# A four-column-tile form for projection and mixer matmuls that follow value matmuls, with a planned order, in a two-layer attention-and-mixer kernel

## The chip, the cores and the metric

The kernel runs on one core of one Trainium2 chip. The time is device microseconds of one execution, and lower is better. Each profile gives the granted clock of TensorE (PE). PE multiplies matrices, ACT (ScalarE) evaluates exponentials and gelus, DVE (VectorE) copies and normalises, and the program gives each engine its own queue of instructions. Where the text below says "at equal clock", it compares single runs of two kernels whose granted clocks are nearly the same.

## The reference, cut to what matters

```python
x = A_x                                           # 1 x 2048 x 448
x = x + attention(layernorm(x), wqkv, wo)         # 16 heads of 28
x = x + B(layernorm(x), w1, w2, w3, w4)
x = x + attention(layernorm(x), wqkv, wo)         # same weights again
x = x + B(layernorm(x), w1, w2, w3, w4)

# B: h = gelu(layernorm(x) @ w1); four quarters of h shifted by +1, -1, +2, -2 rows;
#    x1 = x + shifted(h) @ w2;  x1 + gelu(layernorm(x1) @ w3) @ w4     (w3: 448 x 1792)
```

The softmax needs 2 x 16 x 2048 x 2048 exponentials. They are ACT's work and the largest single item of the kernel.

## The kernel before

The program writes tasks (Python generators); a scheduler picks, operation by operation, what each engine does next, and so fixes the order of every engine's queue before anything runs. Rows of x go in 16 tiles of 128. The scores of a "granule" (3 or 2 banks of PSUM, alternately) are computed by PE, one exponential instruction turns them into the tile PT, and value matmuls multiply PT with V. Scores for granule n+2 can start only after exponential n has read its banks.

Score matmuls use tiles of 32 rows of the array, value matmuls tiles of 32 columns, and all other matmuls the whole array ("plain"):

```python
# scores: contraction over 32 rows, tile at row r0
yield op("pe", ..., lambda e, ...: e.matmul(out=ps[:, bk, :], lhsT=kT[r0:r0 + rn, g, kc:kc + 128],
    rhs=qT[r0:r0 + rn, g, q0:q0 + 512], ..., tile_position=(r0, 0)), ..., mode="r%d" % rn, dl=0.55)
# values: four heads j, 32 columns each
yield op("pe", ..., lambda e, ...: e.matmul(out=ps[32 * j:32 * j + 32, UBK, 0:128 * nt],
    lhsT=vaug[:, vs, 32 * (4 * g + j):32 * (4 * g + j) + 32], rhs=rhs, ..., tile_position=(0, 32 * j)), ..., mode="col4")
# a mixer matmul, plain: w3
for (fc, rows) in KCM:
    yield op("pe", c_mm(NW), lambda e, ...: e.matmul(out=ps[:, bi(b), 0:NW],
        lhsT=w3[0:rows, fc, 128 * fch:128 * fch + 128], rhs=xt.v[0:rows, 0:n, fc, :], ...), ...)
```

The greedy rule, with fixed priorities, and the fillers. A filler is a plain matmul whose result nobody reads. It is put where the scheduler expects PE to be idle, so that PE keeps its clock (e10 below, with 330 fillers fewer than after, spent 109 us at half clock against 20):

```python
key = (ready if eng == "act" else start, t[0], t[1])      # earliest start, then task priority
# ... cut ...
def keep_pe_busy(self, until):
    while self.cur["pe"] + dur + 0.12 < until:            # dur = 0.13: ident @ wv, 256 columns
        # ... cut: a free bank, at most 80% busy over the last 4 us ...
        self.P.add("pe", lambda e, b=pick: fn(e, b), reads, [key(pick)], t_end=t + dur)
```

The shifted quarters are kept in hT, a ring of 8 tiles. A mixer task for tile t may write its slot when the tile that held it is done with. "Done" is signalled only at the end of that tile's whole mixer:

```python
def t_mixA(L, tiles, direct):
    for t in tiles:
        for tp in (t - HR - 1, t - HR, t - HR + 1):       # HR = 8
            if 0 <= tp < NT:
                yield ("wait", ("mixBt", L, tp))
# t_x1: ps = shifted(hT) @ w2: the last reader of hT.   Then w3, gelu, w4, and only then
                yield ("sig", ("x2", L, t))
                yield ("sig", ("mixBt", L, t))
```

## Time and profile before

| what | before |
|---|---|
| time, median (4 runs) | 1169.1 us (1163.9 to 1169.3) |
| span of the profiled run | 1167.1 us, granted clock 0.980 |
| ACT busy / idle | 1047.7 / 119.4 us |
| exponentials | 821 instructions, 940.2 us |
| first exponential starts / last one ends | 27.9 / 1080.9 us |
| PE busy, of which fillers | 1091.1, 168.2 us |

From the page of the kernel before: busy time of the engines with share of the span and number of instructions, then three rows of the span in 40 slices (tenths busy; PEclk is the granted clock in tenths).

```profile
PE 1091.1 (93%) x7799; PEld 406.0 (35%) x7799; DVE 649.7 (56%) x1566; ACT 1047.7 (90%) x955; POOL 58.4 (5%) x76
PE   4899999989999999998999999998999999899998
ACT  5799999999999999994999999998889999999144
PEclk9999999999999999999999999998779999999999
```

PE looks like the busiest engine, but its busy time contains fillers, as the group of line 1302 shows. In a group's line the columns are: line, engine, operation, output and inputs, count, busy time and mean ns of one, idle time of the engine just before and what ended it.

```profile
L955 ACT ACTIVATE PT<-ps 128x1536 bf16<-128x1536 f32 (+1 forms) x821 | 940.2, 1258 | 45.9 <-PE ps L932 37.7
L1302 PE MATMUL ps<-wv,ident 128*128 128x256 bf16 x1102 | 168.2, 279 | 8.8 <-DVE kT L704 2.2
```

So ACT sets the floor, and its idle time is what can be won. The table by stage of the kernel before, cut at the first and at the last exponential, shows where that time lies: us from the span's start and length, then the busy time (and count) of each engine, the clock, DMA share and GB/s.

```profile
0.00:27.90 27.90, 12.27 (x73) 4.67 (x73) 21.31 (x82) 13.99 (x21) 12.13 (x18) 1.00 0.76 177
27.90:1080.90 1053.00, 1000.05 (x7110) 350.81 (x7109) 578.04 (x1356) 1005.84 (x875) 40.29 (x47) 0.98 0.12 31
1080.90:1167.10 86.20, 78.82 (x623) 50.55 (x617) 50.33 (x130) 27.90 (x61) 5.99 (x11) 1.00 0.11 30
```

ACT, the fourth engine in each row, is idle for 13.9 us ahead of the first exponential, about 47 us between the first and the last, and 58.3 us in the tail of 86.2 us. The largest gap in the middle is the change of layers. ACT's timeline there (start, length, what; in brackets the idle time before and what ended it):

```profile
539.18 0.60 ACT L955 ACTIVATE PT<-ps 128x512 bf16<-128x512 f32 x1
556.01 2.37 ACT L955 ACTIVATE PT<-ps 128x1024 bf16<-128x1024 f32 x2 [16.24 <-PE ps L932]
```

The tail is long because the mixer runs late. The chain that ended last, in order of time, still holds the w3 matmuls, the gelu and the w4 matmuls of tiles 7 to 10 after the last exponential:

```profile
1094.80 12.28 PE ps L1239 x56
...
1107.89 6.19 ACT h2T L1254
...
1114.12 10.77 PE ps L1259 x56
```

What a change of shape costs PE is read from the starts of its matmuls. A plain matmul of 512 columns is followed by the next after 216 ns. Where the next one is of another kind (row tiles, column tiles, plain), a further 95 to 105 ns pass, in every pairing. Leaving out pairs with one of the small matmuls of the softmax's normalisation, 1,807 such changes are in this trace: about 180 us of PE.

### The profile page before, as it was taken

What the parts mean: (1) busy time and instruction counts of PE and PEld (TensorE: products, weight loads), DVE (VectorE), ACT (ScalarE), POOL (GpSimd) and SP (SyncE); (2) the same over time, 40 slices, a digit from 0 to 9 for tenths busy, and PEclk for the clock granted to TensorE, in tenths of its full rate; (3) what the DMA queues carried; (4) which work ended last, traced back from release to release, by engine and by line L of the source; (5) the groups of instructions that cost most, each with busy time, mean ns of one, the idle gap of its engine ahead of it and who ended that gap; (6) DMA issues with size and microseconds to landing.
All of it is one profiled execution on the core that took longest, in us unless ns stands there. A gap on an engine that the chain in (4) does not pass through costs nothing.

```text
span 1167.1 us, 18576 instructions
## 1 busy us (share of the span) xinstructions
PE 1091.1 (93%) x7799; PEld 406.0 (35%) x7799; DVE 649.7 (56%) x1566; ACT 1047.7 (90%) x955; POOL 58.4 (5%) x76
## 2 busy tenths in 40 slices
PE   4899999989999999998999999998999999899998
PEld 1222333333332323334233323332333333333565
DVE  7876356523573255734767462557542574447952
ACT  5799999999999999994999999998889999999144
POOL 4000000000010000000001000000000010001000
PEclk9999999999999999999999999998779999999999
DMA  7122160000000000000111112321000110010011
GB/s 170 37 82 64 32 157 19 15 1 19 19 18 2 19 19 19 12 8 19 28 37 42 28 46 63 83 55 45 10 15 1 31 28 1 1 31 14 23 31 35
DMA packets 79213, 40.18 MB, mean 34 GB/s; under 512 B 63960, under 2 KB 72536, under 8 KB 79128
## 3 DMA queue, kind: packets, MB, share of 16 engines
q1 hardware_dynamic: 77544, 36.23, 12.2%
q0 software_dynamic: 1584, 2.75, 0.8%
q8 instruction: 61, 1.00, 0.3%
q14 instruction: 24, 0.20, 0.1%
HBM read 13.75 MB, written 8.13 MB: 19 GB/s over the span
## 4 chain that ended last, share of the span: by engine, by line
ACT 44%; PE 39%; DVE 14%; DMA 1%; issue 1%; POOL 0%; SPq 0%; DVEq 0%
ACT PT L955 38%; PE ps L932 9%; PE ps L979 7%; PE ps L1259 5%; PE ps L1239 4%; PE ps L1302 4%; ACT h2T L1254 4%; PE ps L695 3%; PE ps L756 2%; PE ps L1118 2%; DVE x1b L1194 1%; PE ps L715 1%; PE ps L1050 1%; DVE x_res L1197 1%; DVE st L1199 1%
## 5 line engine op out<-in xcount | busy, mean ns | idle before, releaser
L955 ACT ACTIVATE PT<-ps 128x1536 bf16<-128x1536 f32 (+1 forms) x821 | 940.2, 1258 | 45.9 <-PE ps L932 37.7
L932 PE MATMUL ps<-qT,kT 32*128 32x512 bf16 (+1 forms) x2048 | 335.8, 392 | 13.8 <-ACT PT L955 9.1
L979 PE MATMUL ps<-PT,vaug 128*32 128x512 bf16 (+1 forms) x2304 | 232.5, 368 | 3.1 <-ACT PT L955 1.8
L1302 PE MATMUL ps<-wv,ident 128*128 128x256 bf16 x1102 | 168.2, 279 | 8.8 <-DVE kT L704 2.2
L932 PEld LDWEIGHTS ps<-qT,kT 32*128 32x128 bf16 (+1 forms) x2048 | 79.4, 91 | 253.7 <-ACT PT L955 176.2
L1248 DVE CAST h2T<-ps 128x512 bf16<-128x512 f32 (+2 forms) x126 | 73.9, 586 | 113.0 <-PE ps L1239 112.2
L1239 PE MATMUL ps<-xT,w 128*128 128x512 bf16 (+3 forms) x672 | 129.0, 311 | 0.3
L1302 PEld LDWEIGHTS ps<-wv,ident 128*128 128x128 bf16 x1102 | 93.5, 99 | 82.3 <-issue 45.7
L1259 PE MATMUL ps<-w,h2T 128*128 128x448 bf16 x448 | 101.0, 358 | 11.4 <-ACT h2T L1254 11.4
L979 PEld LDWEIGHTS ps<-PT,vaug 128*32 128x32 bf16 x2304 | 57.2, 94 | 125.8 <-issue 88.6
L1262 DVE TENSOR_TENSOR x_res<-x_res,ps 128x448 f32<-128x448 f32 x32 | 19.8, 618 | 120.5 <-PE ps L1259 120.5
L1239 PEld LDWEIGHTS ps<-xT,w 128*128 128x128 bf16 x672 | 49.6, 97 | 58.4 <-issue 32.3
L1254 ACT ACTIVATE h2T<-h2T 128x7168 bf16<-128x7168 bf16 (+2 forms) x9 | 45.1, 5015 | 20.2 <-DVE h2T L1248 20.1
L1259 PEld LDWEIGHTS ps<-w,h2T 128*128 128x128 bf16 x448 | 38.7, 98 | 60.1 <-issue 19.5
L994 DVE COPY u_sb<-ps 128x512 f32<-128x512 f32 (+1 forms) x36 | 22.7, 629 | 37.1 <-PE ps L979 36.1
L1118 PE MATMUL ps<-xT,w 128*112 128x512 bf16 (+2 forms) x160 | 40.8, 364 | 0.6 <-DVE x1b L1194 0.6
L695 PE MATMUL ps<-xT,wk_pad 128*128 128x512 bf16 x128 | 39.8, 398 | 1.1 <-DVE qT L739 0.8
L695 PE MATMUL ps<-xT,wq_pad 128*128 128x512 bf16 (+1 forms) x144 | 38.6, 369 | 0.8 <-DVE qT L739 0.7
L1067 DVE TENSOR_SCALAR hT<-ps 112x512 f16<-112x512 f32 (+1 forms) x32 | 21.0, 655 | 31.0 <-PE ps L1118 31.0
L998 DVE SCALAR_TENSOR_TENSOR u_sb<-uin,fct,ps 128x512 f32<-128x512 f32 x24 | 17.9, 747 | 36.1 <-PE ps L979 34.2
L1050 PE MATMUL ps<-wo_pad,otn 128*128 128x448 bf16 x128 | 35.8, 362 | 2.0 <-DVE x_res L1054 1.3
L620 DVE BATCH_NORM_STATS2 st<-x_res 128x6 f32<-128x448 f32 x60 | 37.0, 618 | 1.0
(138 smaller groups left out, 852.0 us busy)
## 6 DMA issues: line engine op xcount, KB each, us to landing
uscr<-u_sb SPq DMA_DIRECT2D x24, 256.0 KB, 2.7
uin<-uscr SPq DMA_DIRECT2D x24, 256.0 KB, 2.8
x_res<-in_A_x_dram POOLq DMA_DIRECT2D x3, 896.0 KB, 12.0
out_dram<-uin SPq DMA_DIRECT2D x16, 112.0 KB, 1.7
w<-in_B_w_dram SPq DMA_DIRECT2D x1, 1568.0 KB, 15.6
w<-in_B_w_dram SPq DMA_DIRECT2D x1, 1344.0 KB, 10.7
h2T<-in_A_wqkv_dram SPq DMA_DIRECT2D x2, 336.0 KB, 6.5
xT<-xn SPq DMA_TRANSPOSE x37, 3.6
```

The lines of the kernel that those rows point to most:

```text
L620: yield op("dve", 0.55, lambda e: e.bn_stats(out=st6[:, t, :], in_=w4[:, t, :] if staged else x_res[:, t, :]), reads=[("w4",) if staged el ...
L695: yield op("pe", c_mm(nw), lambda e, fc=fc, rows=rows, b=b: e.matmul(out=ps[:, bi(b), 0:nw], lhsT=wpad[0:rows, fc, 128 * g:128 * g + 128], ...
L932: yield op("pe", 0.225 if k == 0 else 0.005 if nt == 4 or k == 1 else 0.215, lambda e, bk=bk, r0=r0, rn=rn, g=g, kc=kc, q0=q0: e.matmul(ou ...
L955: yield op("act", 0.077 + 0.427 * cnt, lambda e, b0=b0, p0=p0, cnt=cnt: e.activation(out=PT[:, p0:p0 + cnt, :], in_=ps[:, b0:b0 + cnt, :], ...
L979: yield op("pe", 0.055 if nt == 4 else 0.035, lambda e, j=j, rhs=rhs, vs=vs, i=i: e.matmul(out=ps[32 * j:32 * j + 32, UBK, 0:128 * nt], lh ...
L1050: yield op("pe", c_mm(D), lambda e, g=g, tt=tt, b=b: e.matmul(out=ps[:, bi(b), 0:D], lhsT=otn[:, g, 128 * tt:128 * tt + 128], rhs=wo_pad[: ...
L1118: yield op("pe", c_mm(NW), lambda e, fc=fc, rows=rows, grp=grp, b=b: e.matmul(out=ps[0:112, bi(b), 0:NW], lhsT=w1[0:rows, fc, 112 * grp:11 ...
L1239: yield op("pe", c_mm(NW), lambda e, fc=fc, rows=rows, fch=fch, b=b: e.matmul(out=ps[:, bi(b), 0:NW], lhsT=w3[0:rows, fc, 128 * fch:128 * ...
L1248: yield op("dve", c_ps(NW), lambda e, fch=fch, b=b: e.tensor_copy(out=h2T[:, fch, hoff:hoff + NW], in_=ps[:, bi(b), 0:NW]), reads=[("ps", ...
L1254: yield op("act", c_act(14 * NW), lambda e: e.activation(out=h2T[:, :, hoff:hoff + NW], in_=h2T[:, :, hoff:hoff + NW], func=ACT.Gelu_apprx ...
L1259: yield op("pe", c_mm(D), lambda e, fch=fch, i=i, b=b: e.matmul(out=ps[:, bi(b), 0:D], lhsT=h2T[:, fch, hoff + 128 * i:hoff + 128 * i + 12 ...
L1302: SC.fill = (0.13, lambda e, b: e.matmul(out=ps[:, bi(b), 0:256], lhsT=ident[:, :], rhs=wv[:, 0, 0:256], start=True, stop=True), ["b6", "b ...
```

## The change

Its stated intent: a projection or mixer matmul that follows a value matmul is issued as four matmuls of 32 columns each, in the four column tiles, so that the array's mode does not change. The difference between the two programs holds more than that:

1. the four-column form;
2. ring slots of hT that count as free once the x1 matmuls have been issued ("x1"), not after w4 ("mixBt");
3. projections and mixer matmuls split into independent tasks per group (`par`);
4. scores of the two-tile units in four 32-row tiles, where they used two 64-row tiles;
5. a plan: the schedule is built, latest starts are computed backwards, and it is built again with them as priorities, twice; then 193 fixed random perturbations of these priorities (the recorded texts below say 200; the list in the kernel has 193 numbers);
6. some changed duration constants and rules in the scheduler. Among them, a filler may use any of the eight PSUM banks that holds nothing live, where it had two banks.

The core of the diff, with cuts marked:

```diff
+        def mm(nw, m, dst, lhs, rhs, start, stop, **kw):
+            def whole(e):
+                return e.matmul(out=dst(0, m), lhsT=lhs(0, m), rhs=rhs, start=start, stop=stop)
+            def cols4(e):
+                return [e.matmul(out=dst(a, min(m, a + 32)), lhsT=lhs(a, min(m, a + 32)), rhs=rhs,
+                                 start=start, stop=stop, tile_position=(0, a)) for a in range(0, m, 32)]
+            return op("pe", c_mm(nw), whole, cols=cols4, **kw)
...
                         m = kw.get("mode", "plain")
+                        if self.pe_mode == "col4" and "cols" in kw:
+                            m, dur, fn = "col4", dur + self.COLT, kw["cols"]
...
-                key = (ready if eng == "act" else start, t[0], t[1])
+                key = (ready if eng == "act" else max(start, self.cur[eng] + self.EPS) if eng in ("pe", "dve") else start, ranks[k])
...
+    def latest_starts(self, total):      # cut: backwards over all operations
+def reorder(plan, seed):                 # cut: shifts some tasks of the plan by random amounts
...
-                        yield ("wait", ("mixBt", L, tp))
+                        yield ("wait", ("x1", L, tp))
...
-            for fch in range(14):
+            def w3_group(fch):
...
+            yield from par(prio, [w3_group(fch) for fch in range(14)])
...
+        plan = None
+        for k in range(ROUNDS):          # 2
+            res = attempt(plan)
+            plan = res[2].latest_starts(res[0])
+        for seed in SEEDS:               # 193 numbers
+            plan = reorder(plan, seed)
+        est, P, SC = attempt(plan)
```

## The prediction

> **What bounds the kernel now.** The page gives ACT 1047.7 us busy (90%) and PE 1091.1 us, but 168 us of PE are fillers, so ACT sets the floor: exponentials 940.2 us, gelu 45.1, tanh 20.1, direct gelus 11.6, table loads about 20. Its 119 us of idle time can be won. The ACT timeline places it: about 15 us before the first exponential (27.9 us); about 50 between that and the last (1081 us), of which 16.2 in one gap at 540 us between the layers, 11 at 803-870 us and 9 at 34-110 us; about 58 in the 86 us tail.
>
> **Why.** At 540 us and in the tail ACT waits for mixer work that ran late. In the chain that ended last the 4-tile gelu stands at 1108-1114 us, its second matmuls follow, and only their addition at 1117 us starts the last tiles' mixer. That is the ring of hT: slots come free by "mixBt", signalled after w4, although the x1 matmuls read hT last, long before. In the 803-870 us stretch the granted clock was 0.75 (table by stage).
>
> **Mode changes, from matmul starts.** Unchanged, a 512-column matmul follows after about 216 ns; a change of shape (32-row, four-column, plain) adds 95-105 ns in every pairing. The Trainium skill, "TensorEngine Tiling (Array Packing)", Key Properties, says that changing the mode drains the engine; the trace agrees and gives the size. I count about 1,800 changes, 180 us of PE. About 190 are between value and plain matmuls, about 100 between value matmuls and fillers; the rest enter or leave score matmuls and stay.
>
> **The change, costed.**
> - Four-column form: removes 190 x 0.1 = 19 us of PE, perhaps 25 with more work placed behind value matmuls. It costs about 12 ns a group (starts 3.5 ns apart): on some 500 matmuls, 6 us. Net 13-19 us of PE, mostly hidden behind ACT: worth about 5 us. The value matmuls already stream at 217 ns per group with 94 ns loads hidden, so I expect no load cost.
> - The last two units' scores use four 32-row tiles for two 64-row: about 10 us of PE off.
> - Slots freed at x1, independent groups, latest-start priorities from planned passes: mixer batches run beside attention in place of the 152 us of fillers outside the tail. Gap at 540: 16 to about 3 us. Other gaps 35 to about 22. Tail: the batch of tiles 7-10 (12.3 + 6.2 + 10.8 us in the chain) and part of the next leave it; the last three tiles remain, about 23 us of PE and 20 of latency: 86 to about 44 us. Moved gelus and table loads, about 12 us, delay the last exponential.
> - ACT work: unchanged.
>
> **Sum.** 1169 - 13 - 13 - 42 + 12 = about 1113; I say 1114 us, range 1090 to 1144. Faster by over 2% 0.90, within 2% 0.08, slower 0.02.
>
> **What would show each step.** ACT busy within 10 us of 1048, idle about 65. Last exponential 1060-1080 us; tail 40-50 us without a 4-tile gelu. Gap between layers below 6 us. Value-to-plain changes near zero; matmul instructions up by well over 1,000; filler time down by a third or more. One four-column group of 512 columns follows another after 215-230 ns.
>
> **What would make it wrong.** The order is tuned on modelled durations; where the chip differs, in-order queues turn small errors into ACT waits: 1130-1145. The clock halves where PE looks idle: fewer fillers, or narrow tiles counting as less activity, could bring more 0.75 stretches. If the mixer still lags, the tail stays. If four loads per group don't hide, crowded stretches slow. Better: in-stream idle near zero gives 1090.

## The result, and the profile after

The kernel after takes 1121.3 us (median of 4 runs, 1113.2 to 1121.6) against 1169.1: 48 us less. The ratio is 0.9585, with a 95% interval of 0.9534 to 0.9635. A ratio is the mean time of one kernel's runs over that of the other's of the same rounds, so it is not quite the ratio of the medians quoted. In another job (run e12 below) the same kernel took 1113.6 us.

The page of the kernel after, the same rows:

```profile
PE 1054.9 (94%) x9097; PEld 418.1 (37%) x9097; DVE 615.7 (55%) x1531; ACT 1053.1 (94%) x968; POOL 56.3 (5%) x76
PE   4999999999999999999999999999999999999998
ACT  4899999999999999998999999999999999989944
PEclk9999999999999999999999999999999999979999
```

ACT works as much as before (1053.1 us); its idle time fell from 119.4 to 66.7 us. The two groups that answer to those of before:

```profile
L1122 ACT ACTIVATE PT<-ps 128x1536 bf16<-128x1536 f32 (+1 forms) x821 | 937.3, 1254 | 16.3 <-PE ps L1096 9.1
L1475 PE MATMUL ps<-wv,ident 128*128 128x256 bf16 x1154 | 178.2, 280 | 4.0 <-DMA wv<-in_A_wqkv_dram 2.4
```

ACT's wait for scores fell from 37.7 to 9.1 us, while filler time rose a little. The table by stage of the kernel after, cut at its own first and last exponential (40.1 and 1070.7 us):

```profile
0.00:40.10 40.10, 24.80 (x138) 11.75 (x138) 28.82 (x99) 21.54 (x34) 13.95 (x20) 1.00 0.58 134
40.10:1070.70 1030.60, 987.63 (x8564) 377.56 (x8563) 558.75 (x1357) 1012.51 (x882) 37.88 (x48) 0.99 0.13 32
1070.70:1119.80 49.10, 42.42 (x399) 28.79 (x397) 28.08 (x77) 19.09 (x54) 4.48 (x8) 0.99 0.13 34
```

The sum is exact: the head is 12.2 us longer, the middle 22.4 us shorter, the tail 37.1 us shorter, together 47.3 us, which is the difference of the spans. The head is the least firm of the three: in e12, the same kernel again, the first exponential starts at 37.0 us. The gap between the layers, in ACT's timeline after:

```profile
516.30 11.41 ACT L1122 ACTIVATE PT<-ps 128x1536 bf16<-128x1536 f32 x10
533.29 2.37 ACT L1122 ACTIVATE PT<-ps 128x1536 bf16<-128x1536 f32 x2 [5.58 <-PE ps L1146]
```

16.2 us have become 5.6. The 4-tile gelu that stood in the tail now runs between exponentials, on the same timeline at its end:

```profile
1042.35 1.28 ACT L1422 ACT_TABLE_LOAD   x1
1043.64 6.18 ACT L1422 ACTIVATE h2T<-h2T 128x7168 bf16<-128x7168 bf16 x1
...
1065.93 4.74 ACT L1122 ACTIVATE PT<-ps 128x1024 bf16<-128x1024 f32 x4 [0.25 <-PE ps L1146]
1075.62 0.58 ACT L1464 ACTIVATE uin<-x_res 128x448 bf16<-128x448 f32 x1 [4.95 <-DVE x_res L1430]
```

Changes of mode on PE fell from 1,807 to 1,636. Value-to-plain went from 153 to 0 and plain-to-value from 37 to 8. In all, 330 matmuls took the form (1,320 narrow ones).

Part of the gain came with a higher clock. The profiled run of before spends 47 us at half clock, that of after 20. Most of the 47 us lie in one stretch of before:

```profile
803.00:870.00 67.00, 63.25 (x386) 20.54 (x374) 40.16 (x106) 55.97 (x50) 3.02 (x4) 0.75 0.11 26
```

The 46 exponentials that start in it take 67.1 us, with ACT idle for 11.0; the same 46 take 56.6 us in after, at a clock of 0.97 and with ACT idle for 1.7. To bound the whole effect, take the run of before with the most clock (1161.5 us at 0.988, of 35 runs in all jobs) and the run of after with the least (1121.1 us at 0.990): 40 us remain. So some 8 us of the 48 came with the clock, and no experiment says which part of the change raised it.

The total is what was forecast. Which of the six parts made it is another question, and the parts cannot be told apart in these two traces.

### The profile page after: what moved, and what is told of

It is laid out like the page before. It is cut to its first block, busy times and chain, and to the rows that moved or that the text cites. A ratio compares the mean times of both kernels' runs of the same rounds, so it can differ in the third digit from the quotient of the medians.

```text
span 1119.8 us, 21130 instructions
## 1 busy us (share of the span) xinstructions
PE 1054.9 (94%) x9097; PEld 418.1 (37%) x9097; DVE 615.7 (55%) x1531; ACT 1053.1 (94%) x968; POOL 56.3 (5%) x76
## 3 DMA queue, kind: packets, MB, share of 16 engines
q8 instruction: 71, 1.16, 0.4%
## 4 chain that ended last, share of the span: by engine, by line
ACT 80%; PE 16%; DVE 2%; DMA 1%; issue 0%; SPq 0%; ACTq 0%; DVEq 0%
ACT PT L1122 73%; PE ps L646 8%; ACT h2T L1422 4%; PE ps L1096 3%; PE ps L1146 2%; PE ps L1475 1%; ACT gt L1243 1%; PE ps L649 1%; DMA wv<-in_A_wqkv_dram 1%; ACT L1422 1%; ACT L1122 1%; DMA xT<-xn 0%; DVE hT L1234 0%; ACT h2T L1412 0%; DVE h2T L1415 0%
## 5 line engine op out<-in xcount | busy, mean ns | idle before, releaser
L1122 ACT ACTIVATE PT<-ps 128x1536 bf16<-128x1536 f32 (+1 forms) x821 | 937.3, 1254 | 16.3 <-PE ps L1096 9.1
L1096 PE MATMUL ps<-qT,kT 32*128 32x512 bf16 (+1 forms) x2304 | 322.7, 362 | 23.7 <-ACT PT L1122 17.8
L1475 PE MATMUL ps<-wv,ident 128*128 128x256 bf16 x1154 | 178.2, 280 | 4.0 <-DMA wv<-in_A_wqkv_dram 2.4
L1096 PEld LDWEIGHTS ps<-qT,kT 32*128 32x128 bf16 x2304 | 81.0, 91 | 265.8 <-ACT PT L1122 145.4
L646 PE MATMUL ps<-xT,w 128*128 128x512 bf16 (+6 forms) x698 | 128.0, 310 | 2.2 <-DVE h2T L1415 0.4
L646 PE MATMUL ps<-w,h2T 128*128 128x448 bf16 x369 | 83.8, 354 | 9.4 <-ACT h2T L1422 9.0
L646 PEld LDWEIGHTS ps<-xT,w 128*128 128x128 bf16 (+1 forms) x698 | 54.6, 103 | 51.9 <-issue 23.3
L649 PE MATMUL ps<-xT,w 128*32 128x512 bf16 (+3 forms) x536 | 43.9, 353 | 0.0
L781 DVE BATCH_NORM_STATS2 st<-x_res 128x6 f32<-128x448 f32 x60 | 36.7, 613 | 1.6 <-DMA x_res<-in_A_x_dram 0.8
L1371 POOL TENSOR_TENSOR mst<-mst,neghalf 128x1 f32<-128x1 f32 x32 | 19.6, 620 | 345.3 <-DVE mst L1369 345.3
L1268 POOL TENSOR_TENSOR mst<-mst,neghalf 128x4 f32<-128x4 f32 (+2 forms) x10 | 9.6, 965 | 508.8 <-DVE mst L1267 508.8
L646 PE MATMUL ps<-xT,wq_pad 128*128 128x512 bf16 (+1 forms) x113 | 29.8, 367 | 2.0 <-DVE qT L864 0.5
```

Of the source, the lines that this page charges most:

```text
L646: return e.matmul(out=dst(0, m), lhsT=lhs(0, m), rhs=rhs, start=start, stop=stop)
L649: return [e.matmul(out=dst(a, min(m, a + 32)), lhsT=lhs(a, min(m, a + 32)), rhs=rhs, start=start, stop=stop, tile_position=(0, a)) for a i ...
L781: yield op("dve", 0.55, lambda e: e.bn_stats(out=st6[:, t, :], in_=w4[:, t, :] if staged else x_res[:, t, :]), reads=[("w4",) if staged el ...
L1096: yield op("pe", 0.005 if ph == h else 0.012 + W / 2400.0, lambda e, bk=bk, r0=32 * j, g=g, kc=kc, q0=q0, W=W, c0=W * h: e.matmul(out=ps[: ...
L1122: yield op("act", e_dur(n), lambda e, b0=b0, p0=p0, cnt=cnt: e.activation(out=PT[:, p0:p0 + cnt, :], in_=ps[:, b0:b0 + cnt, :], func=ACT.E ...
L1371: yield op("pool", 1.0, lambda e, t=t: e.tensor_tensor(out=mst[:, t, R3:R3 + 1], in0=mst[:, t, V3E:V3E + 1], in1=neghalf[:, 0:1], op=ALU.pow),
```

## The experiments

Two theories at the start. Theory S, mine: the earlier mixer (freed slots, plan) makes the gain, and the form is mostly hidden behind ACT. Rival F: the form makes it. The runs came from five chip jobs: before and after, e1 to e4, e5 to e8, e9 and e10, e11 and e12. The kernel before ran in each (medians 1166.4 to 1169.7 us). After ran in two of them, 7.7 us apart, so differences of a few us across jobs carry little. Beside each is the span of its profile, split as above into head (before the first exponential), middle and tail:

| run | median us | ratio to before | head / middle / tail of its profile |
|---|---|---|---|
| before | 1169.1 | 1 | 27.9 / 1053.0 / 86.2 |
| after | 1121.3 | 0.9585 | 40.1 / 1030.6 / 49.1 |
| e1 after, same order, whole matmuls | 1152.8 | 0.9869 | 36.7 / 1058.8 / 51.0 |
| e2 before with the form alone | 1158.6 | 0.9927 | 27.0 / 1050.8 / 79.3 |
| e3 before with the freed ring alone | 1161.4 | 0.9937 | 27.4 / 1052.6 / 70.8 |
| e4 after without perturbations | 1140.0 | 0.9764 | 51.0 / 1039.0 / 48.9 |
| e5 e4 without the form | 1151.7 | 0.9880 | 46.4 / 1059.5 / 50.6 |
| e6 e4 with the ring freed late | 1157.6 | 0.9921 | 49.4 / 1054.2 / 49.8 |
| e7 after with no plan at all | 1169.3 | 1.0036 | 50.7 / 1052.6 / 60.7 |
| e8 after, fillers in the mode around them | 1142.8 | 0.9793 | 38.1 / 1059.3 / 50.4 |
| e9 e1 with 330 fillers dropped | 1176.6 | 1.0083 | 37.4 / 1081.7 / 49.4 |
| e10 after with 330 fillers dropped | 1142.5 | 0.9781 | 36.8 / 1051.0 / 49.0 |
| e11 after with 233 more perturbations | 1107.2 | 0.9495 | 36.8 / 1019.5 / 47.8 |
| e12 after once more, same chip as e11 | 1113.6 | 0.9556 | 37.0 / 1024.7 / 49.1 |

All gave correct results. The 95% intervals of the ratios are 0.3 to 0.9% to each side.

### e1: the same order, but whole matmuls

```diff
             def cols4(e):
-                return [e.matmul(...) for a in range(0, m, 32)]
+                return whole(e)
```

The order of the queues stays that of after; only the form is undone.

> The kernel after, same order of all instructions, but every four-column group (330 of them) is issued as one whole 128-column matmul. Theory S (the gain is the mixer's earlier scheduling; mode changes matter little because ACT is the limit): the 171 or so saved mode changes come back, about 17 us of PE, of which most hides behind ACT: 1122 to 1132 us. Rival F (the four-column form is what gives the 48 us): 1150 us or more.

Measured: 1152.8 us (1145.7 to 1154.3). That is rival F's number, and 31 us above after. At equal clock the difference is the same: 1145.7 us at a granted clock of 0.999 here, 1113.2 us at 0.998 there. The stage table of e1 says where it goes: its middle stage lasts 1058.8 us against 1030.6 (1024.7 in e12), and the tail hardly differs. ACT is idle for 37.4 us of that stage, against 18.1 in after.

```profile
36.70:1095.50 1058.80, 1014.75 (x7554) 370.35 (x7573) 560.91 (x1358) 1021.37 (x882) 37.84 (x48) 1.00 0.12 31
```

In this fixed order the whole form is much dearer than I had reckoned. One piece of PE's timeline shows why. The kernel after, between two sets of scores (line 1146 is the value matmul, 649 the four-column form of w4, 1096 the scores):

```profile
395.68 0.60 PE L1146 MATMUL ps<-PT,vaug 128*32 128x512 bf16 x5
395.91 0.36 PE L649 MATMUL ps<-w,h2T 128*32 128x448 bf16 x3
396.10 0.39 PE L1146 MATMUL ps<-PT,vaug 128*32 128x512 bf16 x3
396.12 0.35 PE L649 MATMUL ps<-w,h2T 128*32 128x448 bf16 x1
396.42 0.39 PE L1096 MATMUL ps<-qT,kT 32*128 32x512 bf16 x3
```

The same piece in e1 (line 1145 the value matmul, 646 the whole w4 matmul, 1095 the scores):

```profile
401.22 0.60 PE L1145 MATMUL ps<-PT,vaug 128*32 128x512 bf16 x5
401.76 0.36 PE L646 MATMUL ps<-w,h2T 128*128 128x448 bf16 x1
402.05 0.40 PE L1145 MATMUL ps<-PT,vaug 128*32 128x512 bf16 x3
402.38 0.39 PE L1095 MATMUL ps<-qT,kT 32*128 32x512 bf16 x3
```

From the first value matmul to the scores it takes 0.74 us with the form and 1.16 us without. Two changes of mode, about 0.2 us, are one half of the difference. The other half is sharing. The value matmuls come as four, then one alone, then three. In the first trace three tiles of the w4 group start with that lone value tile, and its last tile starts with the last three value tiles, so that all four column tiles are in use. In the second trace the lone tile and the three tiles each hold the array for themselves. In 119 of the 330 groups some tile starts within 60 ns of a value tile. Over the 128 stretches between scores that hold such groups and no fillers or small matmuls, and whose records are complete in both traces (279 groups), e1 takes 34.8 us longer from scores to scores. Changes of mode rose to 1,894, that is 258 more than after, or about 26 us of PE at 0.1 us each.

### e2: the form alone, in the kernel before

```diff
+                        if self.pe_mode == "col4" and "cols" in kw:
+                            m, dur, fn = "col4", dur + 0.012, kw["cols"]
...   (and mm(...) in the place of each projection and mixer matmul)
```

> The kernel before with the four-column form alone, in its own greedy scheduler (a projection or mixer matmul behind a value matmul takes the form). Theory S: 0 to 10 us faster than before, 1159 to 1169 us, gap at the layer boundary and tail of about 86 us still there. Rival F: most of the 48 us, 1120 to 1135 us.

Measured: 1158.6 us, ratio 0.9927. This is 9 us below the 1167.4 us of before in the same job, theory S's number. At equal clock less is left: e2's four runs (clocks of 0.982 to 0.987) lie 2 to 4 us below the runs of before at the same clocks. 281 groups took the form and changes fell to 1,624, lower than in after, yet the gap between the layers is still 16.3 us and the tail 79.3. So "the form gives 31 us" holds only in the order of after.

### e3: the freed ring alone, in the kernel before

```diff
-                        yield ("wait", ("mixBt", L, tp))
+                        yield ("wait", ("x1", L, tp))        # "x1" now signalled right behind the x1 matmuls
```

> The kernel before with one change: slots of the ring hT count as free when the x1 matmuls that read them have been issued, not after the second MLP matmul (w4). Theory S, ring part: the mixer runs earlier, tail 86 to some 50-60 us, gap between layers shorter, 1125 to 1150 us. Rival O (it is the planned order, not the freed slots): within 1% of before, 1158 to 1172 us. Rival F: no change.

Measured: 1161.4 us, ratio 0.9937. The ring theory's forecast for this run fails. By the medians of the job the ring gives 6 us; at equal clock it is more, about 10 us (1160.8 and 1162.0 us at 0.972, where four runs of before took 1170.9 to 1172.7). The tail falls from 86.2 to 70.8 us in the profiles, but a 4-tile gelu is still in it, and the gap between the layers (15.1 us) stays. The greedy order has the slots and does not use them in time.

### e4: no perturbations

`SEEDS = []`; the two planning rounds stay.

> The kernel after without the 200 random perturbations of the plan; the two planning rounds stay. Theory S: the structure (freed slots, groups, latest starts) gives most of it, 1125 to 1145 us. Rival O2 (the searched order is what counts): above 1150 us.

Measured: 1140.0 us. Structure, form and plan without any search give 29 of the 48 us, the perturbations the other 19. Of these, by the table, 11 us lie in the head (first exponential at 51.0 against 40.1 us; 37.0 in e12), 8 in the middle and none in the tail.

### e5, e6, e7: one part taken from e4 (or from its plan)

e5, the form taken out and the order planned without it:

```diff
-            return op("pe", c_mm(nw), whole, cols=cols4, **kw)
+            return op("pe", c_mm(nw), whole, **kw)
```

> The kernel after without the perturbations (as in the run without seeds, 1140 us) and without the four-column form, so that the planner may order for whole matmuls. Theory T (the form is worth what the order makes of it: undone in a fixed order it cost 31 us, but an order planned without it loses less): 1142 to 1155 us. Rival F2 (the form itself is worth some 30 us whatever the order): 1165 us or more.

Measured: 1151.7 us, 12 us above e4, as theory T has it. Its profile has 41 us of half clock and e4's 14, so a part of the 12 is the clock's. The single runs give its size: the run of e5 with the most clock took 1149.0 us at 0.991, the run of e4 with the least 1141.0 us at 0.993. Of these 8 us about 2 go with the clock (e5's own runs differ by about 1 us for each 0.001), so about 6 us are left for the form, an estimate across two jobs.

e6, e4 with the ring freed after w4 again:

> The kernel after without the perturbations, four-column form kept, but with the ring hT's slots counted as free only after w4, as before. Ring theory: the mixer of later tiles waits again, tail 65 us or more, 1155 to 1175 us. Rival (planned priorities alone bring the mixer forward, the ring hardly matters, as its 6 us alone in the kernel before suggest): within 6 us of 1140 us.

Measured: 1157.6 us, 18 us above e4. The time is as the ring theory expected and its place is not: the tail stays at 49.8 us, and the loss lies in the middle (1054.2 against 1039.0 us), where ACT waits more. Its waits, in e4 (first) and in e6 (second; both on the scores and the value matmuls):

```profile
ACT PT L1110 <- PE ps L1084: 15.5, 14, 4.0
ACT PT L1110 <- PE ps L1134: 3.3, 3, 1.6
```

```profile
ACT PT L1110 <- PE ps L1134: 17.7, 9, 4.6
ACT PT L1110 <- PE ps L1084: 16.7, 16, 4.5
```

That the late slots hold up the mixer between exponentials is the likely reading; no run looked further.

e7, no planning rounds (`ROUNDS = 0`, `SEEDS = []`), all else as after:

> The kernel after with no planning rounds and no perturbations: fixed priorities as before, but freed slots, independent groups, four-column form, 32-row scores for the half units. If planning is the main part: 1150 us or more, tail 65 us or more. If structure and form are: 1145 us or less.

Measured: 1169.3 us, no faster than before. The tail is 25.5 us shorter than before, but the first exponential starts 22.8 us later, and a gap of 17.0 us at the change of layers is still there. With the plan (e4) that gap is 4.0 us. So without a plan the parts take as much as they give, and with it they give 29 us. At equal clock e7 is even the slower one: 1174.0 us at 0.984, where before took 1162.4 to 1164.1.

### e8: fillers that keep the mode

If changes of mode delay scores, fillers should not change it either. In the finished order a run of fillers between score and value matmuls takes the form of the matmul before it (or, if that has none, after it):

```diff
+            if m == "col4":     # four 32-column tiles
+                return [e.matmul(out=ps[a:a+32, bi(b), 0:256], lhsT=ident[:, a:a+32], rhs=wv[:, 0, 0:256], ...) for a in range(0, 128, 32)]
+            return e.matmul(out=ps[:, bi(b), 0:256], lhsT=ident[0:32, :], rhs=wv[0:32, 0, 0:256], ..., tile_position=(0, 0))
```

> The kernel after, same order, but a run of fillers that stands between score and value matmuls takes the form of the matmul before it (four 32-column tiles, or one 32-row tile), so that it changes no mode. If mode changes delay scores in the crowded stretches: about 300 changes fewer, ACT waits for scores down from 9 us to some 4, 1114 to 1120 us. Rival H (narrow fillers count as less activity): more half-clock time than the 20 us of after, and 1125 us or more.

Measured: 1142.8 us, 21 us slower than after; rival H. From 110 to 200 us, where fillers are many, the stage table of e8 (first) and of after (second) reads:

```profile
110.00:200.00 90.00, 86.30 (x650) 32.98 (x651) 35.35 (x79) 78.65 (x68) 2.02 (x2) 0.70 0.27 70
```

```profile
110.00:200.00 90.00, 85.85 (x696) 32.38 (x694) 45.74 (x106) 89.97 (x82) 2.02 (x2) 1.00 0.26 71
```

The granted clock (third from the right) is 0.70 against 1.00, and ACT loses 11 us. Over the whole trace the half clock holds for 157 us against 20. The Trainium skill, "TensorE: Matmul & The Clock Gate", Part 1, says that the clock gate halves the clock by how busy PE has been, in windows of 3.4 us. The records agree: only full and half clock occur, and the half-clock stretches are 3.4 us or multiples of it (but for the last, which the end of the run cuts off).

The busy time of PE in the two lines (86 of 90 us in both) cannot tell whether narrow fillers count for less, because a matmul at half clock is busy for longer (a set of scores lasts 0.61 us at 130 us of e8, 0.39 in after). The windows before a drop can. Cut each trace, from 40 to 1,100 us, into windows of 3.4 us in step with its first drop, and take those at full clock. In before, after, e1 and e12, none of the 1,154 windows with PE busy for 78% or more was followed by half clock, and 11 of the 58 below 78% were. In e8, 7 of the 37 windows between 78 and 86% were followed by it; all seven hold narrow fillers, and none of the 14 without them was. So narrow fillers seem to count for less than their busy time, though the line is not sharp (in e3 and e5, without narrow fillers, 3 of 31 such windows were followed too).

Which of the two new forms is to blame was not separated. Of the changed fillers 591 have the row form and 204 the column form, and the window before the drop at 93 us holds the row form alone. Changes of mode fell to 1,230, so whether that would help at full clock stays open.

### e9 and e10: fillers taken away

Why does PE's time show, when PE has 178 us of fillers? One theory, Q: the fillers are fixed entries of an in-order queue and do not shrink when PE is late. In e9 and e10 each group of the four-column kind takes the next filler behind it out of the queue (330 of 1,154; the waits of a dropped filler move to the next PE instruction). e9 does it to e1, e10 to after.

> As the run with the same order and whole matmuls (1153 us), but each of the 330 former groups takes away the next filler behind it in PE's queue, about 110 ns, as much as a mode change; the waits of the dropped fillers move to the next PE instruction. Theory Q (the fillers are fixed entries of an in-order queue, so PE has no slack to absorb the added changes with; give it back and the time is hidden): 1120 to 1134 us. Rival C (the loss sits in crowded stretches where there is no filler to give): 1146 us or more. Half-clock time above some 40 us would spoil the reading.

> Control: the kernel after, four-column form kept, with the same 330 fillers taken away. Theory Q: PE was not late here, so 1113 to 1123 us, ACT's waits for scores at most the 9 us of after. If the clock falls for want of fillers: more half-clock time than 20 us and 1125 us or more.

Measured: e9 1176.6 us, e10 1142.5 us. Both lost their clock (99 and 109 us at half clock), so by the condition stated beforehand the totals do not decide. The row of the clock on the page of e10:

```profile
PEclk9999999999999999799899998799889988899999
```

A part of the traces can be used. Up to the 164th exponential, about 225 us, neither e9 nor e10 has a half-clock stretch. There, counted from the first exponential, e9 falls 4.0 us behind e10 and 3.9 us behind after. Over the same exponentials e1 falls 3.9 us behind after. The 30 fillers taken out by then (about 3 us) changed nothing, which speaks against Q and for rival C: the time is lost in places where there is no filler to give.

That can be counted in after and e1 directly. Take the time from the start of one exponential to the start of the next as a window, and sort the 820 windows by what PE does in them in the kernel after:

| in the window | windows | e1 longer by, in sum | of them longer by over 0.1 us |
|---|---|---|---|
| a four-column group, no filler | 194 | 24.3 us | 77 |
| a group and a filler | 9 | 0.1 us | 1 |
| fillers, no group | 235 | -1.6 us | 1 |
| neither | 382 | 5.4 us | 24 |

The groups stand where the windows are full, and the fillers stand elsewhere. Scores are only two granules ahead of the exponential, so what PE has free in one window is of no use in another. This is a count in two traces and an argument from the code; no run lengthened the look-ahead of the scores.

### e11 and e12: a faster version

e11 appends 233 further perturbations to the list of 193. They were found by trying new random numbers and keeping those that shorten the planned schedule; no run on the chip was used to choose them. e12 is after itself on the same chip.

> The kernel after with 233 more accepted perturbations of the order behind the 200 it has; nothing else differs. If the search still gains what it gained so far (200 of them: 1140 to 1121 us), but with falling returns: 1106 to 1116 us. Rival (the order is already as good as the chip can tell, later gains are lost in waits that the plan does not know and in half-clock windows): 1117 to 1125 us.

> The kernel after, unchanged, on the same chip as the run with more perturbations, so that the two stand beside each other: 1113 to 1122 us.

Measured: e11 1107.2 us (1105.9 to 1108.2), e12 1113.6 us (1112.5 to 1116.1). The ratios to before are 0.9495 and 0.9556; every run of e11 is below every run of e12. ACT's wait for scores is down to 3.0 us (4.3 in e12), and the middle stage from 1024.7 to 1019.5 us. e11 beats both kernels.

## Why the prediction was right or wrong

The total was right: 1114 us forecast with 1090 to 1144, and 1121.3 measured. The signs it named, point by point:

- ACT work unchanged, busy within 10 us of 1048, idle about 65: right (1053.1 and 66.7 us).
- Last exponential at 1060 to 1080 us, tail of 40 to 50 us without a 4-tile gelu, gap between layers below 6 us: right (1070.7, 49.1, 5.6).
- Value-to-plain changes near zero, well over 1,000 more matmuls: right (0 left; 1,298 more).
- "It costs about 12 ns a group": a group of 448 or 512 columns follows another after 189 or 216 ns, exactly as plain ones do, so the form costs nothing in the stream. This part was too high, in the harmless direction: the 6 us of cost are not there.
- "Filler time down by a third or more": wrong. It rose from 168 to 178 us. The mixer did move beside attention, but it did not displace the fillers.
- Not forecast: the first exponential starts 12.2 us later (9.1 in e12).
- Not forecast: half-clock time fell from 47 to 20 us. The prediction saw the stretch at 0.75 and feared more of them.

The step that failed is the size of the form: "Net 13-19 us of PE, mostly hidden behind ACT: worth about 5 us." Its main error is the overlap. "Mostly hidden behind ACT" does not hold: e1 is 31 us slower, and ACT's idle time in the middle is 37.4 us there against 18.1. The table of windows under e9 and e10 points to why: the groups stand where PE has no filler to give. The gross size was too low as well. In the final order, undoing the form lengthens the stretches that hold 279 of the 330 groups by 34.8 us. The changes avoided were near the upper figure of the prediction (258, about 26 us; it said "perhaps 25"). The cost that it took off is nil, and the sharing of the array between tiles of both kinds was not in it. What the form is worth depends on the order: 9 us in the old one (e2), 12 us where the plan may adapt (e5 against e4), 31 us in the searched one (e1), or some 3, 6 and 32 us at equal clock. The Trainium skill's remark on draining ("TensorEngine Tiling (Array Packing)", Key Properties) was the right thing to build on, and the trace's 95 to 105 ns the right price; what failed was the step from PE's time to the kernel's.

The ring step was right in direction and too simple. "Slots freed at x1" alone gave 6 us (e3; about 10 at equal clock), not most of the tail; under a plan it is worth 18 us (e6), and not in the tail. What shortens the tail from 61 to 49 us and closes the gap between the layers is the plan (e7 against e4). So the sum came out well partly because its mixer terms held as a whole. The rest is luck. The sum has no term for the form: it counts ACT's gaps, whatever closes them, so it could be right while the worth of the form was not. ACT's idle time in the middle (18 us) came out lower than forecast (about 25), 9 us of it in the stretch that was at half clock before; and the later start of the exponentials, which was not forecast either, took 12 us back. The parts interact, and their single effects do not add up to 48 us.

What stays open: what the score tiles, the split into groups and the filler banks (parts 4, 3 and 6) do alone, for which no run was made; which part raised the clock; which filler form of e8 lost it; and whether more banks for scores would make PE's free time usable.

## What to carry to other kernels

When a kernel switches between row-tiled, column-tiled and whole-array matmuls, count the switches in the trace and price them from the starts of matmuls; then issue neighbours of a column-tiled matmul in column tiles too, which also lets them fill columns that a split group leaves idle. Idle or filler time of an engine summed over a kernel is not slack: ask whether it lies in the same window, between the same two waits, as the work in question. And measure a part in the order it will live in: the same form was worth 9, 12 and 31 us in three orders. Compare runs at equal clock before reading a difference of 10 us: of the 9 and the 12 us, about a third and a half were left.

## What the Trainium skill lacked or had wrong

- "TensorEngine Tiling (Array Packing)", Key Properties, says that a change of tiling mode drains the engine but gives no size: here 95 to 105 ns for every pairing of row tiles, column tiles and whole array.
- The same page treats column tiles as a way to pack matmuls of up to 64 columns. It does not say that a full 128-column matmul can be cut into four column tiles at no cost in the stream (189 ns for 448 and 216 ns for 512 columns in both forms).
- The same page, Restrictions, says that column tiling turns fast weight load off. "TensorE: Matmul & The Clock Gate", LDWEIGHTS, gives columns / 1.2 ns, which is 27 ns for 32 columns. The recorded loads of 32 columns last 95 ns and those of 128 columns 97 ns (lines 649 and 646 in the kernel after), but those of 112 columns 129 ns. A recorded load may hold a fixed part, which no run here separates. Back to back the loads of both forms stay hidden behind the stream.
- "TensorE: Matmul & The Clock Gate", Part 1, ties the clock to how busy PE is. It does not say whether matmuls on a part of the array count for less. In e8, 7 of 37 windows with PE 78 to 86% busy were followed by half clock, all with narrow fillers; in before, after, e1 and e12 none of 61 such windows was.
